# A changed machine model inside a self-scheduling attention and state-space kernel: measured load times, port locks, constants on VectorE, tables in idle time, longer softmax hops

## Chip, cores and metric

The kernel runs on one core of one Trainium2 chip. The metric is the device time of one execution in microseconds (us). Executions are repeated, and each comes with the mean clock that was granted to TensorE, as a share of full speed. A comparison uses rounds in which both kernels run on the same chip. A ratio is the mean time of one kernel's runs over that of the other's of the same rounds, with a 95% interval, so it is not quite the ratio of the medians that are quoted. "Faster" and "slower" here mean by over 2%.

## The reference, cut to what matters

Two independent halves are computed, and their outputs are concatenated. The second half is multi-query attention: 32 query heads of size 20 share one key head and one value head, and the sequence has 2048 positions.

```python
# A: a diagonal state space layer (L = 2048, H = P = 640)
Lam_bar = exp(exp(log_dt) * Lam);  B_bar = ((Lam_bar - 1) / Lam)[:, None] * Bmat
h_t = Lam_bar * h_(t-1) + x_t @ B_bar.T;  y = 2 * Re(h @ Cmat.T) + x * Dskip

# B: attention, S = 2048, D = 640, H = 32 query heads of 20, one K head and one V head
q = (x @ wq).reshape(S, 32, 20);  k = x @ wk;  v = x @ wv
p = softmax(q k^T / sqrt(20));    out = (p v).reshape(S, 640) @ wo
```

The scores are 32 x 2048 x 2048 exponentials. The kernel works on them as 2048 score tiles of 128 keys (partitions) by 512 queries, for four heads at a time, in blocks of 64 tiles.

## The kernel before

The kernel is a Python program that contains its own list scheduler. Every operation is declared with an engine, a guessed duration, its dependencies and a priority. The scheduler simulates the engines and writes down one fixed order of instructions for each engine. On the chip each engine then runs its order as written, with semaphores for the dependencies. So a guessed duration changes nothing about an instruction; it changes where the instruction stands.

This is how a load was modelled. `tail` is the time that the issuing engine is held for each call, and `dma_free` holds one timeline for each issuing engine:

```python
        if op.dma_key is not None:
            self.free[eng] = self.t + op.tail * len(op.fns)
            s = max(self.t + 1300.0, self.dma_free.get(eng, 0.0))
            self.dma_free[eng] = s + op.dur
            op.end = max(s + op.dur + 700.0, self.free[eng] + 1700.0) + op.land
...
    def loadT(self, pairs, nbytes, key, **kw):          # a load that transposes
        fns = [lambda e, o=o, i=i: e.dma_start_transpose(o, i) for o, i in pairs]
        return self.dma(fns, nbytes, key, issue=1300.0, **kw)
```

The big loads are issued by SyncE, in the order that the scheduler chose:

```python
        o = self.loadT([(p.xaT[:, c, :], xa[0, 0:1024, 128 * c:128 * c + 128]) for c in range(NC)], 1310720, "xa0", ...)
        self.bt_op = [self.loadT([... 5 pieces of B_re, then of B_im ...]), ...]
        self.ct_op = [self.loadT([... 5 pieces of C_re, then of C_im ...]), ...]
```

Softmax needs a bound for each query that replaces the row maximum. The bounds of a group of blocks are one row per head. VectorE writes them to a small buffer (`brow`), and four small loads, also issued by SyncE, put them into a row of the query tile `QT`. A score matmul of these blocks reads that row, so it has to wait for the loads:

```python
        ev = self.dve(self.ts(p.brow[:, rs, :], bank..., LIFT, 0.0, ALU.add, ALU.min), 620, ...)
        fns = [lambda e, j=j: e.dma_start(p.QT[32 * j + 20:32 * j + 21, at:at + ng, :],
                                          p.brow[8 * j + lo:8 * j + lo + ng, rs, :]) for j in range(4)]
        self.row_op[(qb, half)] = self.dma(fns, 32768, f"row{rs}", deps=[ev] + ..., prio=0, land=500.0)
```

Exponentials go two ways. Most tiles are taken by ScalarE, alternately three and two at a time (1536 and 1024 columns, `PR<-SC`). The rest (`DR`) are made by VectorE and GpSimd with integer arithmetic. How many tiles go each way is decided by the scheduler as it goes.

```python
        ex = self.act(lambda e: e.activation(dst, t[:, 0:512 * n], ACT.Exp, scale=1.0 / UNIT),
                      0.8333 * 512 * n + 64, deps=[op], ..., prio=0.5, ...)
```

The constants were filled by GpSimd. The four projections of V ran in the prologue. The sums of softmax make four hops by DMA before a block can be normalized.

Of the kernel before, what the change touches and what calls it, by code (L numbers as in the profile page):

```python
# [9 lines left out]
ALU = mybir.AluOpType  # L10
# [10 lines left out]
class Op:  # L21
# [3 lines left out]
                 "seq", "land", "dma_key", "idx", "tail", "mode", "load", "late", "port", "after", "due")  # L25

    def __init__(self, eng, fns, dur, deps=(), prio=5, reads=(), writes=(), prev=None, gate=None, hook=None,
                 dma_key=None, land=0.0, tail=0.0, mode="F", load=0.0, port=False):
        self.eng, self.fns, self.dur = eng, list(fns), dur
        self.deps, self.prio, self.prev = list(deps), prio, prev  # L30
        self.reads, self.writes = list(reads), list(writes)
        self.gate, self.hook = gate, hook
        self.dma_key, self.land, self.tail = dma_key, land, tail
        self.mode, self.load, self.late = mode, load, False
        self.port, self.after, self.due = port, [], None
        self.start = self.end = None
        self.seq = self.idx = 0


class Schedule:  # L40
# [14 lines left out]
    LOCK = 60.0  # L55

    def __init__(self):
# [15 lines left out]
        self.port_wanted = False  # L73

# [46 lines left out]
    def begin(self, op, eng):  # L121
# [16 lines left out]
        if op.dma_key is not None:  # L138
            self.free[eng] = self.t + op.tail * len(op.fns)
            s = max(self.t + 1300.0, self.dma_free.get(eng, 0.0))  # L140
            self.dma_free[eng] = s + op.dur
            op.end = max(s + op.dur + 700.0, self.free[eng] + 1700.0) + op.land
        else:
            op.end = self.t + op.dur + op.tail
# [3 lines left out]
        for lag in (0.0, 60.0, 100.0, 110.0, 115.0, 130.0, 150.0, 200.0):  # L148
            self.at(op.end + lag)

    def pick(self, eng):
# [28 lines left out]
        for op in can:  # L180
# [3 lines left out]
            if eng == "pe" and op.mode != self.mode:  # L184
                dur += self.SWITCH
                if p > self.URGENT:
# [212 lines left out]
class Build:  # L399
# [60 lines left out]
    def alloc(self, o):  # L460
# [43 lines left out]
        self.trig = sb(o, "trig", [128, 5, NC], FP32)  # L504
        self.rot = sb(o, "rot", [128, NC, 2, 2], FP32)
# [28 lines left out]
    def act(self, fn, dur, **kw):  # L534
        return self.s.add("act", fn, dur, **kw)
# [19 lines left out]
    def loadT(self, pairs, nbytes, key, **kw):  # L555
        fns = [lambda e, o=o, i=i: e.dma_start_transpose(o, i) for o, i in pairs]  # L556
        return self.dma(fns, nbytes, key, issue=1300.0, **kw)
# [31 lines left out]
    def program(self):  # L589
# [21 lines left out]
        self.outs = 0  # L611
        self.constants()
# [48 lines left out]
    def constants(self):  # L661
        self.zero_op = self.dve(lambda e: e.memset(self.PR[:, 0, 0, :], 0.0), 200, writes=["PR0"], prio=0.1)
        p, P = self, self.pool
        self.c_op = {}

        def many(name, fns, dur):
            prev = None
            key = "E1" if name == "E1a" else name
            for f in fns:
                prev = P(f, dur, writes=[key], reads=[key] if prev else [], deps=[prev] if prev else [], prio=1)  # L670
            self.c_op[name] = prev
        many("ident", [lambda e: e.memset(p.ident[:], 0.0),
                       lambda e: e.affine_select(out=p.ident[:], in_=p.ident[:], pattern=[[-1, 128]],
                                                 compare_op=ALU.not_equal, fill=1.0, base=0,
                                                 channel_multiplier=1)], 300)
        many("wk4", [lambda e: e.memset(p.wk4[:], 0.0)], 500)
        iota_i = p.fr[:, 0, 0, :]
        many("iota", [lambda e: e.iota(iota_i, pattern=[[1, 512]], base=0, channel_multiplier=0),
                      lambda e: e.tensor_copy(p.iota[:], iota_i)], 900)
        many("sel32", [lambda e: e.memset(p.sel32[:], 0.0),  # L680
                       lambda e: e.affine_select(out=p.sel32[:], in_=p.sel32[:], pattern=[[0, 4], [1, 32]],
                                                 compare_op=ALU.not_equal, fill=1.0 / (ALPHA * UNIT), base=-20,
                                                 channel_multiplier=64)], 300)
        many("ones32", [lambda e: e.memset(p.ones32[:], 1.0)], 400)
        many("VP", [lambda e: e.memset(p.VP[:], 0.0), lambda e: e.memset(p.VP[:, :, 20:21], 1.0)], 400)
        fns = [lambda e: e.memset(p.VS[:], 0.0)]
        for k, (_, c) in enumerate(self.SHIFTS):
            fns.append(lambda e, k=k, c=c: e.memset(p.VS[:, k, :, 20:21], c))
        many("VS", fns, 250)
        many("step", [lambda e, k=k, c=c: e.memset(p.step[:, k:k + 1], c * 65537) for k, (c, _) in enumerate(self.SHIFTS)], 100)  # L690
        many("VZ", [lambda e: e.memset(p.VZ[:], 0.0)], 100)
        many("maskM", [
            lambda e: e.memset(p.maskM[:], -1.02),
            lambda e: e.affine_select(out=p.maskM[:], in_=p.maskM[:], pattern=[[1, 8], [0, 4], [-1, 8]],
                                      compare_op=ALU.is_equal, fill=0.0, base=0, channel_multiplier=0),
            lambda e: e.affine_select(out=p.maskM[:], in_=p.maskM[:], pattern=[[0, 8], [-32, 4], [0, 8]],
                                      compare_op=ALU.is_ge, fill=0.0, base=0, channel_multiplier=1),
            lambda e: e.affine_select(out=p.maskM[:], in_=p.maskM[:], pattern=[[0, 8], [32, 4], [0, 8]],
                                      compare_op=ALU.is_ge, fill=0.0, base=19, channel_multiplier=-1)], 450)
        many("mask0", [  # L700
            lambda e: e.memset(p.mask0[:], -1.02),
            lambda e: e.affine_select(out=p.mask0[:], in_=p.mask0[:], pattern=[[-32, 4], [0, 32]],
                                      compare_op=ALU.is_ge, fill=0.0, base=0, channel_multiplier=1),
            lambda e: e.affine_select(out=p.mask0[:], in_=p.mask0[:], pattern=[[32, 4], [0, 32]],
                                      compare_op=ALU.is_ge, fill=0.0, base=19, channel_multiplier=-1),
            lambda e: e.affine_select(out=p.mask0[:], in_=p.mask0[:], pattern=[[0, 4], [1, 32]],
                                      compare_op=ALU.is_equal, fill=0.0, base=-20, channel_multiplier=0)], 300)
        many("E1a", [lambda e: e.memset(p.E1[:], 0.0),
                     lambda e: e.affine_select(out=p.E1[:], in_=p.E1[:], pattern=[[-32, 4]],
                                               compare_op=ALU.not_equal, fill=1.0, base=-20,  # L710
                                               channel_multiplier=1)], 250)
# [13 lines left out]
    def loads(self):  # L725
# [4 lines left out]
        self.wk_op = L(p.wkr[:], p.wk.rearrange("(c p) n -> p c n", p=128), 60000, "wk", eng="act", strided=True,  # L730
                       writes=["wkr"], prio=0)
        self.vec_op = [L(p.vrow[NC * i:NC * i + NC, :], v.rearrange("(c p) -> c p", p=128), 3000, f"vec{i}", eng="act",
                         writes=[f"vrow{i}"], prio=0) for i, v in enumerate((self.log_dt, self.Lre, self.Lim, self.Dskip))]
        wqv = p.wq.rearrange("(c p) n -> p c n", p=128)
        wqd = p.wqf[:, 0:NC * 640].rearrange("p (c n) -> p c n", c=NC)
        self.wqa_op = L(wqd[:, :, 0:96], wqv[:, :, 0:96], 200000, "wqa", eng="act", strided=True, writes=["wqa"], prio=0)
        self.wv_op = L(p.wvr[:], p.wv.rearrange("(c p) n -> p c n", p=128), 60000, "wv", eng="act", strided=True,
                       writes=["wvr"], prio=0)

        self.xn_op = [L(self.natural(tb), xb[0, 512 * tb:512 * tb + 512, :].rearrange("(i p) n -> p i n", p=128), 420000,  # L740
                        f"xn{tb}", writes=[f"xn{tb}"], prio=0) for tb in range(2)]
        for c in range(NC):
            o = self.loadT([(p.xbT[:, c, 1024:2048], xb[0, 1024:2048, 128 * c:128 * c + 128])], 262144, f"xb{c}",
                           writes=[f"xbT2_{c}", f"xbT3_{c}"])
            self.xb_op[(2, c)] = self.xb_op[(3, c)] = o
        self.wq_op = L(wqd[:, :, 96:640], wqv[:, :, 96:640], 700000, "wq", strided=True, writes=["wqb"])
        o = self.loadT([(p.xaT[:, c, :], xa[0, 0:1024, 128 * c:128 * c + 128]) for c in range(NC)], 1310720, "xa0",
# [27 lines left out]
    def kv_steps(self):  # L775
        p = self
        wk4_op = None
        for j in range(4):
            wk4_op = self.dve(lambda e, j=j: e.tensor_copy(p.wk4[:, :, 32 * j:32 * j + 20], p.wkr[:]), 120,
# [4 lines left out]
        for c in range(NC):  # L784
            self.wq0_op = self.dve(lambda e, c=c: e.tensor_copy(dst[:, c, :, 0:DH], src[:, c, 0:4, :]), 120,
# [21 lines left out]
        def kv(tb):  # L807
# [3 lines left out]
            for c in range(NC):  # L811
# [10 lines left out]
            kt = self.act(lambda e, src=bank.ap: e.activation(p.KT[:, 512 * tb:512 * tb + 512], src, ACT.Copy, scale=ALPHA * UNIT), 600,  # L822
                          deps=[red], reads=[bank.key], writes=[f"KT{tb}"], prio=0.45)
# [4 lines left out]
            yield lambda: any(x in self.early for x in self.free_banks)  # L828
            bank = self.take(self.early)
            prev = None  # L830
            for i in range(4):
                tk = 4 * tb + i
                prev = self.pe([self.mm(bank.cols(32 * i, 32 * i + 20), p.xbT[:, c, 128 * tk:128 * tk + 128],
# [1041 lines left out]
```

## Time and profile before

| | before |
|---|---|
| time, median of 3 runs | 786.22 us (785.99 to 786.46) |
| time of the profiled run | 783.7 us, granted clock 0.998 |
| span of the profile | 782.0 us |
| first exponential starts | 24.75 us |
| last exponential ends | 770.44 us |
| time in exponentials in between | 737.8 us |
| ScalarE idle in between | 7.9 us |
| tail after the last exponential | 11.53 us |

ScalarE is 96% busy, and its exponentials hold most of the chain, so only three things can move the time: when the exponentials start, how many ScalarE has, and how long it idles between them.

The timeline of ScalarE alone, kernel before (start, duration, engine, line, operation, tiles, count; in brackets the idle time before the row and what ended it):

```profile
24.75 10.49 ACT L1068 ACTIVATE PR<-SC 128x1536 bf16<-128x1536 f32 x9 [0.29 <-PE SC L571]
35.68 11.54 ACT L1068 ACTIVATE PR<-SC 128x1024 bf16<-128x1024 f32 x10 [0.45 <-PE MB L571]
48.32 51.17 ACT L1068 ACTIVATE PR<-SC 128x1024 bf16<-128x1024 f32 x45 [1.11 <-PE SC L571]
...
706.14 64.30 ACT L1068 ACTIVATE PR<-SC 128x1024 bf16<-128x1024 f32 x57 [0.17 <-PE MB L571]
```

Start, idle times and end of the exponentials are read here. The sum of the gaps between these rows is the idle time of the table.

The timeline of the last part of the prologue, kernel before (VectorE and TensorE rows):

```profile
20.38 0.38 PE L571 MATMUL SC<-ones,sel 32*128 32x512 bf16 x1
...
20.48 1.28 DVE L818 TENSOR_REDUCE mab<-SC 128x1 f32<-128x512 f32 x2
...
21.98 0.29 DVE L585 TENSOR_SCALAR M<-mask,mab 128x128 bf16<-128x128 f32 x1
...
22.45 0.40 PE L571 MATMUL MB<-aq,M 128*32 128x512 bf16 x4
...
24.31 0.60 PE L571 MATMUL SC<-QT,KT 32*128 32x512 bf16 x5
```

The last key projection ends at 20.8 us, the maximum of the keys at 21.8 us, the matrix M built from it follows at once, and the first scores start at 24.31 us.

### The profile page before, as it was taken

To read this page: it belongs to the slowest core of one execution; us is meant where nothing else is said; L and a number is where in the kernel's file an instruction comes from. 1 tells how busy PE (TensorE), PEld (TensorE's weight loads), DVE (VectorE), ACT (ScalarE), POOL (GpSimd) and SP (SyncE) were. 2 spreads that over 40 slices of the span, in tenths; PEclk is the share of its full clock that TensorE was granted. 3 is DMA by queue.
4 is the path that set the end of the run, shared out by engine and by line. 5 is a ranking of instruction groups with operands and counts; after the bars stand their busy time and mean duration, and the time that the engine had idled before them with its cause. 6 is when DMAs were issued, how large, how long until landed. Compare 5 with 4: busy or idle time off the path is not lost.

```text
span 782.0 us, 24237 instructions
## 1 busy us (share of the span) xinstructions
PE 731.7 (94%) x10475; PEld 245.0 (31%) x10475; DVE 654.7 (84%) x1193; ACT 754.3 (96%) x675; POOL 444.7 (57%) x460
## 2 busy tenths in 40 slices
PE   8989998998999999989999999989999999999998
PEld 3322222322233333323233223323222322333333
DVE  5989898999988888888989868987789788856995
ACT  5999999999999999999999999999999999999995
POOL 6066566346555556566654754655773456578661
PEclk9999999999999999999999999999999999999999
DMA  9740200000001000020000000110000000010001
GB/s 213 129 78 9 51 9 8 10 3 9 9 10 24 20 18 24 16 43 17 13 12 18 27 16 17 29 29 17 9 16 9 24 23 15 22 30 23 9 9 36
DMA packets 54186, 21.60 MB, mean 28 GB/s; under 512 B 43464, under 2 KB 54080, under 8 KB 54080
## 3 DMA queue, kind: packets, MB, share of 16 engines
q1 hardware_dynamic: 52072, 19.87, 11.7%
q8 instruction: 83, 1.36, 0.7%
q10 hardware_dynamic: 2008, 0.18, 0.2%
q14 instruction: 23, 0.19, 0.1%
HBM read 7.20 MB, written 5.50 MB: 16 GB/s over the span
## 4 chain that ended last, share of the span: by engine, by line
ACT 66%; PE 25%; DVE 5%; DMA 1%; SPq 1%; issue 1%; POOL 0%; ACTq 0%; DVEq 0%; POOLq 0%
ACT PR L1068 66%; PE MB L571 10%; PE MB L567 8%; PE SC L571 7%; DVE DR L586 1%; DMA vrow<-in_A_Dskip_dram 1%; PE SC L567 1%; SPq L556 1%; DVE QT L918 1%; DMA xaT<-in_A_x_dram 0%; DVE VS L585 0%; DVE xbT L797 0%; DVE WO L720 0%; DVE aq L585 0%; DVE fr L586 0%
## 5 line engine op out<-in xcount | busy, mean ns | idle before, releaser
L1068 ACT ACTIVATE PR<-SC 128x1536 bf16<-128x1536 f32 (+1 forms) x650 | 737.4, 1340 | 8.6 <-PE MB L571 5.2
L581 POOL TENSOR_TENSOR DR<-DR,step 128x512 int32<-128x512 int32 x421 | 430.8, 1046 | 315.0 <-DVE DR L586 114.9
L586 DVE TENSOR_SCALAR DR<-MB 128x512 int16<-128x512 f32 x423 | 282.7, 684 | 79.2 <-PE MB L571 74.8
L571 PE MATMUL SC<-QT,KT 32*128 32x512 bf16 x1625 | 253.9, 384 | 35.4 <-ACT PR L1068 25.6
L571 PE MATMUL MB<-DR,VS 128*32 128x512 bf16 x1692 | 225.8, 385 | 2.5 <-DVE pvsb L1337 1.1
L571 PE MATMUL MB<-PR,VP 128*32 128x512 bf16 x1625 | 225.5, 385 | 0.7 <-DVE pvsb L1337 0.3
L571 PE MATMUL MB<-QT,KT 32*128 32x512 bf16 x423 | 154.1, 384 | 2.7 <-DMA QT<-brow 1.8
L571 PEld LDWEIGHTS SC<-QT,KT 32*128 32x128 bf16 x1625 | 64.4, 91 | 268.6 <-ACT PR L1068 178.7
L586 DVE TENSOR_SCALAR DR<-DR 128x1024 int16<-128x1024 int16 (+1 forms) x222 | 83.5, 425 | 7.8 <-PE MB L571 5.6
L571 PEld LDWEIGHTS MB<-PR,VP 128*32 128x32 bf16 x1625 | 57.0, 94 | 66.4 <-issue 49.3
L571 PEld LDWEIGHTS MB<-DR,VS 128*32 128x32 bf16 x1692 | 55.9, 94 | 65.9 <-issue 35.2
L567 PE MATMUL MB<-xaT,BT 128*32 128x512 bf16 x800 | 57.8, 382 | 1.0 <-DMA xaT<-in_A_x_dram 1.0
L581 DVE TENSOR_TENSOR prod<-MB,Z 128x1024 bf16<-128x1024 f32 x40 | 48.7, 1218 | 7.3 <-PE MB L567 6.6
L571 PE MATMUL MB<-xbT,wqf 128*32 128x512 bf16 x640 | 49.0, 387 | 0.7 <-DVE brow L586 0.5
L571 PEld LDWEIGHTS MB<-QT,KT 32*128 32x128 bf16 x423 | 36.3, 91 | 22.0 <-DVE DR L586 10.4
L571 PE MATMUL MB<-KT,VZ 128*32 128x256 bf16 x796 | 41.6, 275 | 0.0
L567 PE MATMUL MB<-WO,OT 128*32 128x128 bf16 (+1 forms) x928 | 40.8, 292 | 0.0
L1633 DVE TENSOR_TENSOR_SCAN g<-sc,hst,u 128x512 bf16<-128x512 f32 x30 | 40.7, 1364 | 0.0
L581 DVE TENSOR_TENSOR prod<-g,tab 128x1024 bf16<-128x1024 bf16 x40 | 32.7, 819 | 0.0
L567 PE MATMUL MB<-CT,xbT 128*32 128x512 bf16 (+1 forms) x640 | 31.2, 300 | 0.1
L567 PE MATMUL MB<-CT,W 128*32 128x512 bf16 (+1 forms) x640 | 29.4, 300 | 0.5 <-issue 0.5
L1456 DVE CAST stg<-MB 128x512 bf16<-128x512 f32 x35 | 23.9, 684 | 5.9 <-PE MB L567 5.6
(124 smaller groups left out, 386.3 us busy)
## 6 DMA issues: line engine op xcount, KB each, us to landing
out_dram<-stg SPq DMA_DIRECT2D x35, 128.0 KB, 1.7
rdB<-recs SPq DMA_DIRECT2D x124, 32.0 KB, 1.9
CT<-in_B_x_dram SPq DMA_DIRECT2D x2, 640.0 KB, 5.6
WO<-in_B_wo_dram SPq DMA_DIRECT2D x4, 200.0 KB
wqf<-in_B_wq_dram SPq DMA_DIRECT2D x1, 680.0 KB, 5.3
out_dram<-PR SPq DMA_DIRECT2D x5, 128.0 KB, 1.9
sums<-pvsb SPq DMA_DIRECT2D x31, 4.0 KB
dn<-sums SPq DMA_DIRECT2D x31, 4.0 KB, 1.9
```

The lines of the kernel that those rows point to most:

```text
L556: fns = [lambda e, o=o, i=i: e.dma_start_transpose(o, i) for o, i in pairs]
L567: r = e.matmul(out[32 * j:32 * j + 32], lhsT=lhsT[:, 32 * j:32 * j + 32], rhs=rhs, start=start, stop=stop, tile_position=(0, 32 * j), skip ...
L571: return lambda e: e.matmul(out, lhsT=lhsT, rhs=rhs, start=start, stop=stop, **kw)
L581: return lambda e: e.tensor_tensor(out, a, b, op)
L586: return lambda e: e.tensor_scalar(out, a, s1, s2, op0=op0, op1=op1)
L918: ev = self.dve(lambda e: e.tensor_copy(dst, bank.ap), 600, deps=[prev], reads=[bank.key], writes=[key], prio=self.EV)
L1068: ex = self.act(lambda e: e.activation(dst, t[:, 0:512 * n], ACT.Exp, scale=1.0 / UNIT), 0.8333 * 512 * n + 64, deps=[op], reads=[b.key fo ...
L1456: ev = self.dve(lambda e: e.tensor_copy(st, bank.ap), 620, deps=[prev], reads=[bank.key], writes=[key], prio=self.EV, gate=(lambda: last.e ...
L1633: o = self.dve(lambda e, ri=ri, init=init: e.tensor_tensor_scan(p.g[:, u, ri, :], rdec, p.u[:, ri, :], init, ALU.mult, ALU.add), 1280, por ...
```

## The change

The change has three parts. The results stay the same; engines, order, the shape of some V projections and the model of the scheduler change.

1. The prologue is modelled with measured times: one shared timeline for all loads, measured sizes of the loads, 1450 to 1930 ns for each transposing load in place of 1300, the time of a table load on ScalarE (1280 ns), and more operations are held to a rule of the model, that VectorE and GpSimd take turns at one port. The four vectors are loaded first.
2. Work is moved: constants go from GpSimd to VectorE, the small scalings `VS` of V from VectorE to GpSimd, the last key eviction from ScalarE to VectorE, the table loads to idle time of ScalarE, and two of the four V projections behind the first scores.
3. Each of the four hops of the softmax sums is modelled 2000 ns longer (`LATE_DMA`).

The core of the diff, with cuts:

```diff
+    TABLE = 1280.0
...
-            s = max(self.t + 1300.0, self.dma_free.get(eng, 0.0))
-            self.dma_free[eng] = s + op.dur
+            s = max(self.t + 1300.0, self.dma_free.get(eng, 0.0), self.pipe)
+            self.dma_free[eng] = self.pipe = s + op.dur
...
-        return self.dma(fns, nbytes, key, issue=1300.0, **kw)
+        return self.dma(fns, nbytes, key, issue=issue, **kw)          # default 1450.0
...
-        many("VP", [lambda e: e.memset(p.VP[:], 0.0), lambda e: e.memset(p.VP[:, :, 20:21], 1.0)], 400)   # on GpSimd
+        many("VP", [fill(p.VP[:], 0.0, 280), fill(p.VP[:, :, 20:21], 1.0, 100)])                          # on VectorE
...
-        self.wk_op = L(p.wkr[:], ..., 60000, "wk", eng="act", ...)
-        self.vec_op = [L(p.vrow[...], v..., 3000, f"vec{i}", eng="act", ...) for i, v in ...]
+        self.vec_op = [L(p.vrow[...], v..., 30000, f"vec{i}", eng=("act", "sp")[i % 2], ...) for i, v in ...]
...
-        o = self.loadT([(p.xaT[:, c, :], ...) for c in range(NC)], 1310720, "xa0",
+        o = self.loadT([(p.xaT[:, c, :], ...) for c in range(NC)], 780000, "xa0", issue=1930.0,
...
-            kt = self.act(lambda e, ...: e.activation(p.KT[...], src, ACT.Copy, scale=ALPHA * UNIT), 600, ...)
+            if tb < 3:
+                kt = self.act(...)
+            else:
+                kt = self.dve(self.ts(dst, src, ALPHA * UNIT, None, ALU.mult), 650, ...)
...
+            if tb < 2:
+                ... V projection in the prologue ...
+            else:
+                self.tasks.insert(0, (-90 + tb, 0, lambda: self.started, lambda bank: self.v_task(tb, bank)))
...
-                vs = self.dve(self.ts(p.VS[...], p.VP[...], c, None, ALU.mult), 120, ...)
+                vs = self.pool(self.ts(p.VS[...], p.VP[...], c, None, ALU.mult), 300, ...)
...
+    LATE_DMA = 2000.0
...
-        o = self.dma(lambda e: e.dma_start(sums, ...), 4096, f"sum{slot}", deps=[ev], ...)
+        o = self.dma(lambda e: e.dma_start(sums, ...), 4096, f"sum{slot}", land=self.LATE_DMA, deps=[ev], ...)   # and three more
...
+        self.act(lambda e: e.activation(p.tload[:], p.tload[:], ACT.Exp), 230, table="exp", deps=tabs + ..., ...)
```

## The prediction

> **What bounds the kernel now.** ScalarE's exponentials. In the groups the 650 exponentials take 737.4 us of the 782.0 us span, with only 8.6 us of idle time before them; in the chain of waits they hold 66%. The timeline gives three parts: a prologue until the first exponential at 24.75 us, 745.7 us of exponentials (to 770.4 us), and a tail of 11.5 us. TensorE is 94% busy, partly with keep-alive fillers.
>
> **What the change does.** It changes the order that the kernel's own scheduler makes.
> - Constants: some 20 fills leave GpSimd (13.9 us busy in the prologue) for VectorE, about 3 us in time it spends waiting for the first loads. Sixteen small VS scalings (2.8 us of VectorE at 22.7 to 26.7 us) go to GpSimd.
> - Loads: the four vectors go first, on two queues. The scalar chain can start near 5 us instead of 8.6 us. Natural x then lands perhaps 0.5 to 1 us later than now (5.6 and 7.6 us).
> - Tables: the exponential table (1.28 us, loaded at 23.17 us) moves ahead of the first scores. It was nearly hidden: the first exponential waited for scores after it, so this is worth under 0.3 us. The Trainium skill, "ScalarE: Activation LUTs", section "What ACT_TABLE_LOAD costs", gives about 1283 ns for a load; the trace agrees.
> - Two of four value projections move behind the first scores: 160 matmuls 32x20 in place of 40 128x20. From the rate of small matmuls in the tail (48 in about 1 us) I estimate 2 to 3 us of TensorE there and a stall of 0.5 to 1 us for ScalarE.
> - The new order has 648 exponentials, not 650 (five score tiles go to VectorE): 737.4/325 = 2.27 us less.
>
> **The prologue, by hand with traced durations.** The new order puts 9 warm-up matmuls before the vectors' transposition and 13 after, before the transposes of x. They ran 0.43 us each until about 5.9 us and 0.22 us later (the Trainium skill, "TensorE: Matmul & The Clock Gate", Part 1, says that a cold array runs at half rate for its first 3 to 4 us of work; the trace agrees). Hence the transposes of x start at about 8.4 us, not 6.8 us. The key projections then end at about 18.5 to 19.5 us instead of 20.8 us. But VectorE then has a KT eviction (0.67 us) before the maximum and a QT eviction (0.68 us) between the maximum and M0. First exponential: 23.3 us (22 to 24.5), so 1.5 us gained of 24.75.
>
> **Later.** Longer modelled hops reorder the normalizations. VectorE waits only 2.1 us in all for those loads, and ScalarE's idle time is 8.6 us in total, so little can come of it, and new stalls can cost as much. Tail unchanged.
>
> **Sum.** Start -1.5, exponentials -2.3, early stall +0.7, steady state -0.3, tail 0: about -3.5 us of 786.2. Predicted 782.7 us, 8 times in 10 between 778.5 and 786.5. Faster by over 2%: 2%; within 2%: 97%; slower: 1%.
>
> **What would show it.** First exponential at 22 to 24.5 us; exponentials near 735 us; idle before them 7 to 10 us; last exponential about 11.5 us before the end; vector landing under 4 us; the 13 warm-up matmuls delaying the first transposes past 8 us.
>
> **What would make it wrong.** A first exponential at 20 to 21 us (loads earlier, VectorE's evictions hidden), or idle time before exponentials above 12 us.

A remark on its second citation: that a cold array runs at half rate agrees with the trace (0.43 us, then 0.22 us for each matmul). The length agrees less well. In the profile of before, the first matmul started at 1.24 us and the full clock came at 5.97 us, 4.7 us later and not 3 to 4.

## More of the kernel before

The page of the kernel before gives the busy time of each engine with its share of the span and its instructions, the granted clock in 40 slices (tenths), the shares of the chain that ended last, and groups of instructions (line, engine, operation, tiles, count; then busy us and mean ns; then idle time just before them and its main releaser).

```profile
span 782.0 us, 24237 instructions
...
PE 731.7 (94%) x10475; PEld 245.0 (31%) x10475; DVE 654.7 (84%) x1193; ACT 754.3 (96%) x675; POOL 444.7 (57%) x460
...
PEclk9999999999999999999999999999999999999999
...
ACT 66%; PE 25%; DVE 5%; DMA 1%; SPq 1%; issue 1%; POOL 0%; ACTq 0%; DVEq 0%; POOLq 0%
...
L1068 ACT ACTIVATE PR<-SC 128x1536 bf16<-128x1536 f32 (+1 forms) x650 | 737.4, 1340 | 8.6 <-PE MB L571 5.2
...
L571 PE MATMUL MB<-QT,KT 32*128 32x512 bf16 x423 | 154.1, 384 | 2.7 <-DMA QT<-brow 1.8
```

## The result and the profile after

| | before | after |
|---|---|---|
| time, median of 4 runs each | 786.34 us (785.99 to 787.09) | 782.50 us (780.68 to 783.20) |
| ratio | | 0.9946 (0.9928 to 0.9965) |
| profiled run, granted clock | 783.7 us, 0.998 | 783.2 us, 0.998 |
| span | 782.0 | 781.1 |
| first exponential | 24.75 | 25.62 |
| time in exponentials | 737.8 | 735.4 |
| ScalarE idle between them | 7.9 | 8.5 |
| tail | 11.53 | 11.64 |

The kernel is 0.5% faster, well within the 2%. Note that the two profiled runs differ by only 0.5 us, while the medians differ by 3.8 us. The profiled run of before was 2.6 us faster than the median of its runs, and that of after 0.7 us slower. Whoever explains the 3.8 us from the two profiles alone explains the wrong 0.5 us.

The page after, the same parts:

```profile
span 781.1 us, 24633 instructions
...
PE 733.0 (94%) x10668; PEld 247.9 (32%) x10668; DVE 667.5 (85%) x1228; ACT 751.6 (96%) x674; POOL 439.2 (56%) x451
...
ACT 76%; PE 18%; DVE 3%; POOL 1%; DMA 1%; issue 1%; ACTq 0%; POOLq 0%; DVEq 0%
...
L1079 ACT ACTIVATE PR<-SC 128x1536 bf16<-128x1536 f32 (+1 forms) x648 | 735.0, 1350 | 10.4 <-PE MB L581 6.5
...
L581 PE MATMUL MB<-QT,KT 32*128 32x512 bf16 x428 | 156.5, 385 | 0.9 <-DVE DR L596 0.6
```

There are 648 exponentials in place of 650, and the wait for the bound rows is gone from the last line.

The timeline of ScalarE, kernel after:

```profile
25.62 2.37 ACT L1079 ACTIVATE PR<-SC 128x1536 bf16<-128x1536 f32 x2 [1.55 <-PE SC L581]
28.87 48.04 ACT L1079 ACTIVATE PR<-SC 128x1536 bf16<-128x1536 f32 x42 [0.88 <-PE SC L581]
77.54 2.54 ACT L1079 ACTIVATE PR<-SC 128x1536 bf16<-128x1536 f32 x2 [0.63 <-PE SC L581]
...
712.77 56.69 ACT L1079 ACTIVATE PR<-SC 128x1536 bf16<-128x1536 f32 x50 [1.05 <-PE MB L581]
```

The first exponential is later, not earlier, and 0.88 us are lost at 28 us, behind the V projections that were moved there. Their 160 matmuls take 1.58 us in two groups, and between these TensorE is idle for 1.20 us without a wait that the profile shows.

The last part of the prologue, kernel after:

```profile
19.75 1.25 PE L581 MATMUL SC<-xbT,wk 128*128 128x512 bf16 x5
...
20.93 0.39 PE L581 MATMUL SC<-ones,sel 32*128 32x512 bf16 x1
...
21.35 0.69 DVE L818 TENSOR_REDUCE mab<-SC 128x1 f32<-128x512 f32 x1
...
22.03 0.68 DVE L595 TENSOR_SCALAR KT<-SC 128x512 bf16<-128x512 f32 x1
...
22.70 0.68 DVE L929 CAST QT<-MB 128x512 bf16<-128x512 f32 x1
23.30 0.28 DVE L595 TENSOR_SCALAR M<-mask,mab 128x128 bf16<-128x128 f32 x1
...
25.19 0.60 PE L581 MATMUL SC<-QT,KT 32*128 32x512 bf16 x5
```

The last key projection ends at 21.3 us, 0.5 us later than before. Between the maximum and M stand two evictions of 0.68 us each.

### The profile page after: what moved, and what is told of

Same layout as the page of the kernel before. It is cut to its first block, busy times and chain, and to the rows that moved or that the text cites. A ratio compares the mean times of both kernels' runs of the same rounds, so it can differ in the third digit from the quotient of the medians.

```text
span 781.1 us, 24633 instructions
## 1 busy us (share of the span) xinstructions
PE 733.0 (94%) x10668; PEld 247.9 (32%) x10668; DVE 667.5 (85%) x1228; ACT 751.6 (96%) x674; POOL 439.2 (56%) x451
## 4 chain that ended last, share of the span: by engine, by line
ACT 76%; PE 18%; DVE 3%; POOL 1%; DMA 1%; issue 1%; ACTq 0%; POOLq 0%; DVEq 0%
ACT PR L1079 75%; PE MB L581 7%; PE SC L581 6%; PE MB L577 5%; DVE DR L596 1%; DMA wqf<-in_B_wq_dram 1%; POOL DR L591 1%; PE SC L577 1%; DVE prod L591 0%; DVE WO L721 0%; DVE pvsb L1348 0%; DVE prod L595 0%; DVE Z L1590 0%; DVE Z L1597 0%; DVE QT L929 0%
## 5 line engine op out<-in xcount | busy, mean ns | idle before, releaser
L1079 ACT ACTIVATE PR<-SC 128x1536 bf16<-128x1536 f32 (+1 forms) x648 | 735.0, 1350 | 10.4 <-PE MB L581 6.5
L591 POOL TENSOR_TENSOR DR<-DR,step 128x512 int32<-128x512 int32 x414 | 424.1, 1046 | 308.5 <-DVE DR L596 129.7
L581 PE MATMUL MB<-DR,VS 128*32 128x512 bf16 x1712 | 233.9, 386 | 3.0 <-DVE pvsb L1348 1.1
L581 PE MATMUL MB<-PR,VP 128*32 128x512 bf16 x1620 | 218.9, 385 | 0.9 <-ACT PR L1079 0.5
L581 PE MATMUL MB<-QT,KT 32*128 32x512 bf16 x428 | 156.5, 385 | 0.9 <-DVE DR L596 0.6
L596 DVE TENSOR_SCALAR DR<-DR 128x1024 int16<-128x1024 int16 (+1 forms) x248 | 92.7, 425 | 6.5 <-PE MB L581 4.5
L581 PE MATMUL MB<-xbT,wqf 128*32 128x512 bf16 x640 | 46.5, 385 | 1.3 <-DVE xbT L797 0.6
L581 PE MATMUL MB<-KT,VZ 128*32 128x256 bf16 x844 | 43.7, 275 | 0.0
L581 PEld LDWEIGHTS MB<-QT,KT 32*128 32x128 bf16 x428 | 36.7, 91 | 20.3 <-issue 11.7
L591 DVE TENSOR_TENSOR prod<-g,tab 128x1024 bf16<-128x1024 bf16 x40 | 34.9, 872 | 0.0
```

What stands on the lines that cost most here:

```text
L581: return lambda e: e.matmul(out, lhsT=lhsT, rhs=rhs, start=start, stop=stop, **kw)
L591: return lambda e: e.tensor_tensor(out, a, b, op)
L596: return lambda e: e.tensor_scalar(out, a, s1, s2, op0=op0, op1=op1)
```

## The experiments

Two theories follow from the profiles.

- The theory of the prediction: the gain is the 2.4 us of exponentials that went to VectorE, plus what the prologue gives. The start does not fit (it lost 0.9 us), so the fewer exponentials would have to carry nearly all.
- The rival, called theory D in the later texts: in most runs of before, TensorE waits for the bound rows near 47 us, its clock then drops to half for some microseconds, and ScalarE starves. The profiled run of before escaped this by luck. The change removes the wait as a side effect, and that is most of its gain.

There were further theories that fell on the way (the longer hops; a better start; a single early transposing load). The texts say with each run what each theory expected; "before" in them is the kernel before in the same rounds.

### 1. The two kernels again, and the two halves of the change

`r1_before` and `r1_after` are the two kernels unchanged, profiled once more. `e_late_only` is before with only the longer hops:

```diff
-        o = self.dma(lambda e: e.dma_start(sums, ...), 4096, f"sum{slot}", deps=[ev], ...)
+        o = self.dma(lambda e: e.dma_start(sums, ...), 4096, f"sum{slot}", land=2000.0, deps=[ev], ...)   # the four hops alike
```

`e_prologue_only` is after without them:

```diff
-    LATE_DMA = 2000.0
+    LATE_DMA = 0.0
```

> Control: the kernel before, unchanged, against itself. Every theory expects a ratio of 1.000 within 0.2%. It also gives a second trace of before on the chip of these rounds: first exponential near 24.75 us, 650 exponentials, last one about 11.5 us before the end.

> The changed kernel again, on the chip of the others. Its first trace had the first exponential at 25.62 us (0.87 us later than before), 735.0 us of exponentials (2.4 us less), idle time between them 8.8 us (before 8.3). If those parts are all there is, it should be about 1 us faster than before; the record says 3.8 us. Expected: 2 to 4 us faster, and the trace should show where the rest lies (idle time between exponentials, or the tail).

> The kernel before with only the longer modelled hops of the softmax sums. Prologue untouched: first exponential at 24.7 us. The order has 1620 score tiles on ScalarE, as the changed kernel has, before has 1625. Theory A (the gain is the tiles that the new order happens to take off ScalarE): 2 to 3 us faster than before, so all of the gain or more, as the prologue adds nothing. Theory B (the new prologue makes the gain): no difference. Theory C (longer hops remove waits for late loads): idle time between exponentials falls by 2 us or more.

> The changed kernel with the longer hops set back to 0: the new prologue alone. 1623 tiles on ScalarE. Theory A: first exponential at 25.6 us (+0.9), exponentials 0.9 us less, so the same as before within 1 us. Theory B: 3 us or more faster than before. Theory C: as slow as before, with idle time between exponentials as in before.

Measured, on one chip (before 785.38 us):

| run | median us | ratio to before | score tiles on ScalarE | exponentials us | idle between us | first exponential |
|---|---|---|---|---|---|---|
| r1_before | 785.62 | 0.9986 (0.9961 to 1.0011) | 1625 | 738.1 | 10.9 | 24.49 |
| r1_after | 783.01 | 0.9965 (0.9945 to 0.9985) | 1620 | 735.5 | 9.8 | 25.45 |
| e_late_only | 785.57 | 1.0003 (0.9983 to 1.0024) | 1620 | 735.0 | 12.8 | 24.28 |
| e_prologue_only | 780.33 | 0.9939 (0.9913 to 0.9966) | 1623 | 736.8 | 7.8 | 25.47 |

The second halves of the rows (tiles to first exponential) come from the profiled run of each. The hops alone take some 3 us out of the exponentials and give nothing. The prologue alone gives the whole gain, though its first exponential is later than before's. Neither fits the first theory. (The profiled run of e_prologue_only is not a typical one either: 782.93 us at a clock of 0.993, 2.6 us above its median. It has a half-clock episode at 29.8 us, right behind the moved V projections, and one at 729.5 us; three of its other runs took 779.1 to 779.6 us at 0.998.)

The second profile of before (786.8 us, granted clock 0.991) shows what the first did not. The timeline of r1_before, SyncE's queue, TensorE and ScalarE rows:

```profile
37.24 6.52 SPq L556 DMA_TRANSPOSE CT<-in_A_C_re_dram  x5
43.80 2.96 SPq L964 DMA_DIRECT2D QT<-brow  x4
...
46.81 7.06 SPq L556 DMA_TRANSPOSE CT<-in_A_C_im_dram  x5
...
47.97 0.58 PE L571 MATMUL MB<-QT,KT 32*128 32x512 bf16 x1 [2.71 <-DMA QT<-brow]
...
49.68 1.02 ACT L1068 ACTIVATE PR<-SC 128x1024 bf16<-128x1024 f32 x1 [2.71 <-PE SC L571]
```

The rows lie ready in `brow` from about 34 us. SyncE issues their loads only at 43.80 us, because five transposing loads of `C_re` stand ahead of them in its order, each some 1.3 us. TensorE waits 2.71 us for them, then ScalarE 2.71 us for TensorE. Before's first profile has the same wait, 1.76 us, ended at 47.26 us:

```profile
47.26 0.37 PE L571 MATMUL MB<-QT,KT 32*128 32x512 bf16 x1 [1.76 <-DMA QT<-brow]
```

Now the clock. The next fence is the busy time by stretch of r1_before (stretch, its length, busy us with instructions of PE, PEld, DVE, ACT and POOL, then the granted clock, the DMA share and GB/s). The stretches are 3.41 us long, because in the trace's record of the clock every change lies a multiple of 3.413 us after the one before it:

```profile
43.62:47.03 3.41, 1.62 (x23) 0.36 (x15) 2.66 (x5) 3.35 (x3) 2.78 (x4) 1.00 0.23 51
47.03:50.45 3.42, 2.48 (x15) 0.45 (x15) 0.69 (x1) 0.77 (x1) 1.82 (x2) 0.50 0.52 96
50.45:53.86 3.41, 3.41 (x39) 0.91 (x36) 1.94 (x5) 2.48 (x3) 0.00 (x0) 0.50 0.84 102
53.86:57.27 3.41, 3.41 (x39) 1.05 (x39) 2.57 (x6) 2.50 (x3) 1.55 (x2) 0.50 0.29 48
```

After a stretch in which TensorE was busy 1.62 us of 3.41, its clock was half for three stretches, 10.24 us. In the last two of these TensorE is busy all the time, at half its clock, and ScalarE is busy about 2.5 of every 3.4 us. The same view of the first profile of before:

```profile
43.52:46.93 3.41, 1.96 (x27) 0.46 (x19) 3.00 (x5) 3.41 (x4) 2.78 (x3) 1.00 0.18 34
46.93:50.34 3.41, 3.08 (x42) 1.02 (x46) 1.85 (x3) 2.23 (x3) 2.16 (x3) 1.00 1.03 91
```

With 1.96 us of work in its stretch it kept its clock. That is the luck: up to the stall ahead of the 65th exponential, which ends at 100.38 us in this run and at 104.02 us in r1_before, ScalarE idled 2.4 us here and 6.2 us there.

The busy time of a stretch does not decide alone. This first profile has one drop, at 449.7 us for one stretch, after 2.63 us of work in which TensorE was never idle for longer than 0.40 us:

```profile
446.29:449.71 3.42, 2.63 (x27) 0.67 (x24) 3.37 (x5) 3.42 (x4) 2.95 (x4) 1.00 0.00 0
```

The Trainium skill, "TensorE: Matmul & The Clock Gate", Part 1, "What's actually happening", says that this gate of the clock is either full or half, that it is set by the activity in a window of 3413 ns, and that this window is free-running. The trace agrees (episodes of 3.41, 6.83 and 10.24 us, clocks of 1.00 and 0.50 alone; the first change to full clock lies anywhere from 4.16 to 7.15 us in the 14 profiles). A free-running window could catch one and the same order of instructions in one run and not in another. In these two profiles of before, though, the windows start within 0.10 us of each other (43.52 and 43.62 us); what differs is that the rows landed 0.7 us later in r1_before (47.83 against 47.13 us), so that more of its window was idle. Its condition of an "idle window" does not agree word for word: here a window with 47% of work was enough.

### 2. The order of one load, a later load, more fillers, a different count

`x1_rows_first` is before with one edit of the finished order of SyncE: the loads of the bound rows go ahead of the transposing loads of `C_re`. Nothing else moves on any engine.

```diff
                 self.s.run()
+                order = self.s.order
+                ct, row = self.ct_op[0], self.row_op[0, 0]
+                order.remove(ct)
+                order.insert(order.index(row) + 1, ct)
```

`x2_rows_late` is after with the opposite edit (the rows behind `C_re`):

```diff
+                ct, row = self.ct_op[0], self.row_op[0, 0]
+                order.remove(row)
+                order.insert(order.index(ct) + 1, row)
```

`x3_fillers` is before with 24 keep-alive steps ahead of the first matmul that reads the rows; the wait of the data stays, but TensorE works through it:

```diff
+                first = next(i for i, op in enumerate(order) if op.eng == "pe" and "QTr1" in op.reads)
+                for _ in range(24):
+                    ... op = Op("pe", four matmuls of zeros, 0.0, mode="C", reads=["VZ", "KT0"], writes=[bank.key])
+                    order.insert(first, op)
```

`x4_pool1045` is before with one constant of the model changed (GpSimd's time for a tile), so that the count of ScalarE's tiles falls with nothing of the change:

```diff
-    POOL2 = 1040.0
+    POOL2 = 1045.0
```

> The kernel before, the same schedule on every compute engine; only SyncE's queue differs: the first four loads of the bound rows into QT go ahead of the five transposing loads of C_re (as in the changed kernel), not behind them. Theory D (the gain is the removed wait for those rows near 47 us, and the half-clock episode of TensorE that this wait starts): rows land near 38 to 40 us instead of 47 to 48 us, no wait for them, no half-clock episode near 47 us, idle time before 100 us falls from 6.2 us to under 3 us, and the kernel is 3 to 5 us faster than before, mean clock about 0.998. Theory A (only the number of exponentials counts): no difference, as both have 650.

> The changed kernel with the opposite edit: the rows' loads put back behind the C_re loads on SyncE, nothing else. Theory D: rows land near 49 us, TensorE waits 2 us or more for them, a half-clock episode of about 10 us appears near 49 us, and the kernel loses 3 to 5 us against the changed one, so it is as slow as before or 1 us slower (mean clock about 0.992). Theory A: as fast as the changed kernel, 2 to 3 us faster than before.

> The kernel before with 24 more groups of four keep-alive matmuls (about 2.5 us of TensorE) put just ahead of the first matmul that waits for the rows; the wait itself stays. It parts the wait from the clock. If most of the loss is the half clock: the rows still land near 47 us and ScalarE still idles 1 to 3 us there, but no half-clock episode follows, and it is 2 to 4 us faster than before. If the loss is the wait alone: no difference from before, or slightly slower.

> The kernel before with one number of the scheduler's model changed by 0.5% (1040 to 1045 ns for a copy on GpSimd), which means nothing for the chip. The prologue and SyncE's first loads stay as they are. Its order has 1618 score tiles on ScalarE, not 1625. If the count is what the changed kernel owes its fewer exponentials to, by chance: exponentials 3 us less than before in the trace (about 734.5 us), and 2 to 3 us faster if idle time and clock stay the same. If not, no difference.

Measured, on one chip (before 786.22 us):

| run | median us | ratio to before | granted clocks of its runs | rows landed us | half-clock episodes in the profile | exponentials us | idle us |
|---|---|---|---|---|---|---|---|
| x1_rows_first | 781.15 | 0.9942 (0.9923 to 0.9962) | 0.997 to 1.000 | 40.39 | 3.41 us at 118.9 | 737.6 | 5.2 |
| x2_rows_late | 781.82 | 0.9954 (0.9932 to 0.9975) | 0.998 to 1.000 | 49.41 | none before the last us | 735.0 | 7.4 |
| x3_fillers | 782.54 | 0.9959 (0.9939 to 0.9979) | 0.998 to 1.000 | 47.65 | 3.41 us at 450.6 | 737.7 | 7.8 |
| x4_pool1045 | 783.75 | 0.9978 (0.9954 to 1.0002) | 0.991 to 0.998 | 47.27 | 6.83 us at 49.6 | 734.8 | 11.7 |

The eleven runs of before in the same rounds had clocks of 0.991 to 0.996.

Moving one group of loads on one queue gives the whole gain, with before's prologue and before's 1625 tiles. The timeline of x1 (SyncE's queue) and its busy time by stretch:

```profile
36.21 3.09 SPq L968 DMA_DIRECT2D QT<-brow  x4
...
39.34 6.40 SPq L560 DMA_TRANSPOSE CT<-in_A_C_re_dram  x5
```

```profile
40.00:50.00 10.00, 9.80 (x135) 3.21 (x135) 9.66 (x18) 10.00 (x10) 6.42 (x7) 1.00 0.66 113
```

The rows are issued 7.6 us earlier than in r1_before, TensorE does not wait for them, the clock stays at 1.00, and ScalarE is busy for all of 40 to 50 us.

x3 parts the wait from the clock. TensorE's fillers, ScalarE's row and the busy time by stretch, in x3:

```profile
45.54 2.80 PE L580 MATMUL MB<-KT,VZ 128*32 128x256 bf16 x96
...
49.35 3.46 ACT L1077 ACTIVATE PR<-SC 128x1024 bf16<-128x1024 f32 x3 [2.02 <-PE SC L580]
```

```profile
40.00:50.00 10.00, 9.98 (x190) 4.56 (x191) 6.96 (x12) 7.97 (x8) 6.71 (x7) 1.00 0.44 90
```

The rows land as late as in before, and ScalarE waits once, 2.0 us, but the clock stays up, and most of the gain is there (3.7 us of x1's 5.1, by the medians). So the halved clock costs more than the wait that brings it on.

x2 went against theory D as it then stood: with the rows behind `C_re` again, the loss should have come back, and it did not. The reason is in the trace. In before, the 56th score tile is the first to read these rows: it is a tile of VectorE that the scheduler takes ahead from the next block. In after it is the 65th. In x2 the rows land at 49.41 us and the 65th tile's matmul starts at 49.80 us, so they still come in time, by 0.4 us. So the change removes the wait in two ways, and each is enough: the rows go out earlier (after lands them at 42.94 us, before at 47.13), and they are read nine tiles later. The first comes from the model: it now knows that transposing loads hold SyncE for longer, and that alone puts the rows ahead (h_issue_only, below). That the second comes from the shared timeline of the loads, so that the model does not expect the rows too early, is likely but was not tested; e_prologue_only has it too, so the longer hops are not needed for it.

After's own order of SyncE, from its timeline:

```profile
38.94 2.92 SPq L975 DMA_DIRECT2D QT<-brow  x4
41.90 6.71 SPq L566 DMA_TRANSPOSE CT<-in_A_C_re_dram  x5
```

x4 shows what the count of tiles is worth. It has 1618 tiles on ScalarE and 3.3 us less of exponentials than r1_before, as predicted from the count; but TensorE waits 1.5 us for the rows, the clock halves at 49.6 us, and the idle time is 11.7 us. By the medians 2.5 us are gained, by the ratio 1.7 us, and its interval just includes no gain. How the count comes about is chance. When before is compiled with 1039, 1040, 1041 and 1045 ns for this constant, it has 1618, 1625, 1620 and 1618 tiles; after, compiled with the same four, has 1618, 1620, 1628 and 1621. (Only the 1045 of before was run, apart from the kernels themselves.)

### 3. One part of the model alone, and two repairs of the prologue

`h_issue_only` is before with only the longer issue times of the transposing loads:

```diff
-    def loadT(self, pairs, nbytes, key, **kw):
+    def loadT(self, pairs, nbytes, key, issue=1450.0, **kw):
-        return self.dma(fns, nbytes, key, issue=1300.0, **kw)
+        return self.dma(fns, nbytes, key, issue=issue, **kw)          # and issue=1930.0 for x and A_x
```

`p1_late_reorder` is after with the last steps of the prologue reordered by hand: the last key eviction and the QT eviction go behind M, and some V work behind the multiplication by M:

```diff
+                after(m0mul, *early_v)
+                after(self.m0_op, kt3)
+                after(low, self.vp_op[0], self.vp_op[1], qt1, self.mm_op)
+                after(fills[1], *group)
```

`p2_fewer_warm` is after without the 13 warm-up matmuls behind the transposition of the vectors:

```diff
+                for op in [op for op in order if op.eng == "pe" and op.reads == ["PR0"]][9:22]:
+                    order.remove(op)
```

> The kernel before with one part of the change alone: the model's queue time of a transposing load, 1300 ns before, 1930 ns for the 1024-row ones and 1450 ns for the others. The order of the first loads, the constants, the tables and the hops stay as before. The scheduler then puts the loads of the bound rows ahead of three groups of transposing loads, by its own choice. Its order has 1621 score tiles on ScalarE. Theory D (removed wait for the rows and half clock): first exponential near 24.5 us, no wait for the rows, no half clock near 47 us, 4 to 7 us faster than before (779 to 782 us), at least as fast as the changed kernel. If another part of the change is needed: under 2 us faster.

> The changed kernel, steady state untouched, with the end of its prologue reordered after scheduling: on VectorE the QT eviction of the second group, Mm and two VP evictions go behind the clamped QT of the first group, and the last KT eviction behind M0; on TensorE the first value projections go behind the M0 matmuls and the third query projection behind the first scores. If the evictions between the maximum and the first scores hold the first exponential (the prediction's reading): it comes 0.5 to 1 us earlier, at 24.5 to 25.1 us instead of 25.5. If TensorE's key projections hold it: under 0.2 us earlier.

> The changed kernel without its second run of 13 warm-up matmuls, nothing else. The prediction held that these delay the transposes of x (7.9 us in the trace) and with them the prologue. If so: transposes start at 6.5 to 6.7 us and the first exponential comes about 1 us earlier. The rival: the next step waits for the query weights, which land at 9.3 us, and for VectorE's copies of them, so the transposes have slack: first exponential earlier by under 0.3 us.

Measured, on one chip (before 785.99 us):

| run | median us | ratio to before | first exponential us | idle between us | half-clock episodes |
|---|---|---|---|---|---|
| h_issue_only | 783.78 | 0.9968 (0.9944 to 0.9992) | 24.84 | 8.5 | 3.41 us at 81, 126 and 750 |
| p1_late_reorder | 785.00 | 0.9985 (0.9955 to 1.0016) | 24.85 | 12.1 | 3.41 us at 25.5 and 80 |
| p2_fewer_warm | 785.73 | 0.9994 (0.9960 to 1.0027) | 26.02 | 11.5 | 3.41 us at 8.8, 6.83 at 29.2, 3.41 at 80 |

h_issue_only: the issue times alone free before of the episode at 47 us (the rows landed at 38.37 us). The order that results has three other short episodes in its profile, and about half of x1's gain is left: 2.2 us, where theory D had expected 4 to 7. Part of that can be owed to its count of tiles (1621; its exponentials take 735.9 us), so this run shows what moves the rows, and not what the removed episode is worth. This is what a static order by a scheduler is like: each edit of the model deals the cards anew.

p1 gave a wrong result (relative error 0.033). I think that my edit put two evictions of V behind the scalings on GpSimd that read them, so those scaled old data; this was not tested. The instructions and their durations are the same, so I use its times with that reservation. The first exponential came at 24.85 us instead of 25.45 to 25.62: the evictions and the V work that were moved behind M had cost about 0.7 us together. But a stall of 4.3 us near the start follows (ScalarE waits for scores), and the kernel as a whole gains nothing from its earlier start.

p2 was a miss for the view that the 13 warm-ups delay the prologue. The transposes of x do start earlier, at 6.30 us instead of 7.90, but the next step waits. TensorE in the timeline of p2:

```profile
9.28 0.62 PE L584 MATMUL MB<-xbT,wqf 128*32 128x512 bf16 x4 [1.91 <-DMA wqf<-in_B_wq_dram]
```

The query weights land at about 9.2 us, TensorE waits 1.91 us, its clock halves from 8.8 us for 3.41 us, and the first exponential comes at 26.02 us, later than with the warm-ups. In after, the same step ran at 9.41 us without that episode. The warm-ups were filling time that was there anyway, and kept the clock up.

### 4. Both gains together

`x5_late_rows_first` is before with the longer hops (as e_late_only) and the order of loads of x1. If the episode at 47 us is what swallows the gain of e_late_only, the two should add.

> The kernel before with two things alone: the longer modelled hops (1620 in place of 1625 score tiles on ScalarE, 2.4 us of exponentials, which gave nothing by themselves: e_late_only 1.0003) and the loads of the second query block's bound rows issued ahead of the CT transposes (which alone gave 0.9942). Theory D (the half-clock episode after the rows' wait is what before loses, and the fewer exponentials come out once it is gone): rows landed by about 41 us, no wait of TensorE for them, no half-clock episode between 45 and 60 us, exponentials near 735 us, idle time between the exponentials down from 12.8 to 5 to 9 us, and 778 to 782 us, 4 to 8 us below before (ratio 0.990 to 0.995). Rival (the order with the longer hops has stalls of its own, as the one near 243 us in e_late_only, which give back what the fewer exponentials save): idle time stays above 10 us and the ratio is 0.995 to 0.999.

Measured, on one chip (before 785.44 us): 781.89 us, ratio 0.9950 (0.9931 to 0.9969). The rows landed at 40.95 us, TensorE did not wait for them, and there was no episode between 45 and 60 us. Exponentials took 734.9 us, and the idle time was 8.8 us, down from 12.8 as theory D said. But the whole is no faster than x1 alone (0.9942), and the ratio lies at the edge where both expectations meet. The rival was half right too: its stall is there. By stretch, and the row of ScalarE that follows, in x5:

```profile
232.85:236.27 3.42, 2.05 (x21) 0.66 (x18) 3.34 (x7) 3.42 (x4) 1.20 (x2) 1.00 0.01 2
236.27:239.68 3.41, 2.96 (x20) 0.72 (x24) 2.62 (x5) 3.41 (x4) 2.83 (x3) 0.50 0.00 0
```

```profile
244.38 66.58 ACT L1072 ACTIVATE PR<-SC 128x1024 bf16<-128x1024 f32 x59 [3.68 <-PE MB L575]
```

TensorE had little work in one window, waiting for ScalarE (0.42 us) and for a tile of VectorE (0.95 us), its clock was half for two windows, and ScalarE then waited 3.68 us. e_late_only has the same stall, 3.1 us at 245 us, behind a half-clock episode at 242.7 us. The order with the longer hops carries a stall of its own that gives back what its fewer exponentials save, in both kernels that were run with before's prologue.

The fastest medians are e_prologue_only (780.33 us, ratio 0.9939 to before) and x1 (781.15 us, ratio 0.9942), both a little below after's in the same or other rounds (r1_after 783.01 us, ratio 0.9965). The intervals overlap, so it is not shown that they beat after; that they beat before is.

## Why the prediction was right or wrong

The time was right: 782.7 us predicted, 782.5 measured. The sum behind it was right only in part, and two wrong terms cancelled (the start by +2.4 us, the steady state by about -3 us). That the total fits this closely is luck.

| term | predicted us | measured us | by |
|---|---|---|---|
| start | -1.5 | +0.9 | first exponential 24.75 to 25.62; again 24.49 to 25.45 |
| exponentials | -2.3 | -2.4 | 737.8 to 735.4; again 738.1 to 735.5 |
| early stall | +0.7 | +0.9 | wait for scores ahead of 28.87 us |
| steady state | -0.3 | about -3.3 (estimate) | see below |
| tail | 0 | +0.1 | 11.53 to 11.64 |

**Start: wrong.** The step that failed is "The key projections then end at about 18.5 to 19.5 us instead of 20.8 us". They ended at 21.3 us. I moved the whole chain forward with the loads, but between 10 and 20 us TensorE was already busy 9.44 of 10 us in after (9.06 in before): each block of keys took its 1.5 us of TensorE, one after the other, with queries and transposes in between, and an earlier load cannot shorten that. That is read from the profiles; no run tests it alone. The chain of waits (`--critical`) agrees. In before it runs over the last vector (landed at 8.56 us). That load is now out of the way, but the chain of after runs over the query weights instead, which land at 9.28 us (9.75 before), and from 12.3 us on over TensorE without a gap. The other half of this step was right: the two evictions on VectorE stand where I said and push the first exponential back (p1, where they and some V work stand later: 24.85 us). The delay of the transposes by the 13 warm-ups was nearly right as a fact (7.90 us, predicted past 8) but irrelevant: p2 shows that the next step waits for the query weights.

**Loads: right.** The last vector landed at 2.83 us (under 4 predicted; 8.56 before), natural x at 6.46 and 8.80 us (5.61 and 7.61 before, so 0.8 and 1.2 us later; 0.5 to 1 us predicted).

**Constants: right.** They moved off GpSimd (busy 13.9 us of the first 20 before, 7.7 after) to VectorE in time that it had (busy 2.5 us of the first 10 before, 6.9 after, other moved work included). None of this was on the path to the first exponential.

**Tables: right in so far as there was little to gain.** The load took 1.28 us in before and in after, as the Trainium skill, "ScalarE: Activation LUTs", "What ACT_TABLE_LOAD costs", says (about 1283 ns); after's stood at 22.58 us, ended before the scores, and the start was set by other steps.

**Exponentials: right in size, but this is a fact of the compiled order, read by counting.** It has no cause in the change that a reader could use; the scan of a constant and x4 show that the count moves by as much for nothing.

**Early stall and tail: right in size.** Of the 2 to 3 us of TensorE that I put down for the moved V projections, 1.58 us are matmuls and 1.20 us are idle time between them.

**Steady state: wrong, and the largest term.** I wrote that "ScalarE's idle time is 8.6 us in total, so little can come of it". That was the idle time of one run, which was 2.6 us faster than the median of the kernel. In r1_before it was 10.9 us (7.9 us by the same view in the first profile). The episode after the wait for the bound rows, which the change happens to remove, costs 3.8 us of idle time before the 65th exponential (6.2 against 2.4 us in the two profiles of before) when it happens. My estimate of about -3.3 us is what is left of the difference of medians (-3.8 us) when the other terms (+0.9, -2.4, +0.9 and +0.1) are taken out. It is less than the 5 us of x1; after has an episode of its own near 76 us in both profiles (3.41 and 6.83 us), with 1.1 and 1.9 us of idle time behind it. Shown by runs: removing it alone, by one reorder of loads (x1), gives 5 us; avoiding the drop of the clock but not the wait (x3) gives 3.7 us; fewer exponentials with it still there give nothing (e_late_only, which has a stall of its own) or 2.5 us, not clear of none (x4).

The clue was on my desk: the profiled run took 783.7 us at a clock of 0.998, and the timed runs 786 us, and the page listed a wait of 1.8 us for the rows. I counted the wait as too small to matter.

**What stays open.** How little work in a window halves the clock, and why the episode then lasts one, two or three windows. The profiles have 1.96 us without a drop (before, 43.52 us) and 1.97 us with one (after, at 72.95 us), and drops after up to 2.66 us (h_issue_only, at 122.18 us). The episodes of 10.24 us come only behind the wait for the rows. Also, whether the untraced longer runs of before all have this very episode: their granted clocks (39 of 44 timed runs at 0.987 to 0.993; one episode of 10.24 us in 785 us makes 0.9935) and x1's (all six at 0.997 or more) say so, but only traces would show it. The times go with the clock: the five of the 44 runs at 0.996 or more took 781.6 to 784.7 us (median 783.5), the other 39 took 784.2 to 789.6 us (median 786.0). And the part of e_prologue_only's gain that is not the removed episode was not separated.

## What to carry to other kernels

Compare the time and the granted clock of the profiled run with the other runs before reading a small change from it; if it is 0.3% faster than the median, the profile does not show what the median pays for. Look at every wait of TensorE of one to three microseconds on a load, however small its share: here the clock afterwards cost more than the wait (x3 against x1), and either the order of loads on the issuing queue or filler matmuls (96 in x3) can avoid it. Short drops also come without such a wait. In an in-order queue, put small urgent loads ahead of long transposing ones; this scheduler did it by itself once its model knew how long those hold the queue (h_issue_only).

## What the Trainium skill lacked or had wrong

- "TensorE: Matmul & The Clock Gate", Part 1: the table names an idle window as the condition for half clock, and the section on oscillation gives "no PE-idle gaps >~3.4µs" as the rule. Here waits of 1.9 and 2.7 us were enough, and windows of 3.41 us with 0.88 to 2.66 us of TensorE work (26% to 78%) were followed by half clock. A window with 1.96 us of work was not. The page does tell of a kernel whose clock swings because of short idle times between groups of matmuls, but gives no figure for how much work a window must hold. Its rule should say that a window need not be empty.
- The same page: it says nothing of how long a re-throttled array that is busy again stays at half clock, beyond one busy window. In r1_before the clock came back only after three windows (10.24 us), though TensorE was busy 3.41 of 3.41 us in the second and third.
- The same page gives about 25 ns as the least distance of matmul starts, however small. In after, 128 matmuls with 20 columns, spread over four column groups, took 1.21 us in all, 9.5 ns each. The page's own Part 3 has tiles in different groups start about 4 ns apart, so the sentence in Part 1 should be limited to matmuls in one group.
- "DMA: Bandwidth & Descriptors" has the constraints and the bandwidth of transposing loads, but not how long one of this size holds the queue that issues it (in its section on trn3 it has a count of cycles for small tiles of earlier chips). Here five of them held SyncE's queue for 6.4 to 8.7 us (1.3 to 1.7 us each), and in r1_before a small load that was ready at 34 us was issued at 43.8 us behind two such groups.
